# Talking-heads attention and squared-ReLU FFN on one core: reciprocals of row sums and pair copies on GpSimd, a post-mix buffer stored in runs of 35, and a new order of units

## The chip, the cores and the metric

The kernel runs on one core of one Trainium2 chip. The metric is the device time in microseconds of one execution; lower is better. Three executions of the kernel before took 535.64, 533.0 and 532.7 us, median 533.0 us.

## What is computed

Eight batches of talking-heads attention (12 heads, 448 rows, head size 64) are followed by one feed-forward layer (768 to 2048 to 768) over all 3584 rows.

```python
scores = scale * np.matmul(q, k.transpose(0, 1, 3, 2))
scores = np.einsum('bhij,hg->bgij', scores, w_pre)
scores = scores - np.max(scores, axis=-1, keepdims=True)
attn = np.exp(scores)
attn = attn / (np.sum(attn, axis=-1, keepdims=True) + 1e-09)
attn = np.einsum('bhij,hg->bgij', attn, w_post)
attn_out = np.matmul(attn, v)
x = attn_out.transpose(0, 2, 1, 3).reshape(B * S, H * D)
h = np.maximum(x @ w_in, 0.0)
out = h * h @ w_out
```

The heads are mixed before the softmax with `w_pre` and after it with `w_post`. These two mixes join all 12 heads of one query row, and they shape the kernel.

## The kernel before, in words

**Tiles.** The 448 query rows of a batch are cut into 45 chunks of 10 (`CH`), the last one with 8 valid rows. A chunk with its 12 heads is 120 rows, held as two groups of 60 (5 query rows by 12 heads, `PR`), one in partitions 0 to 63 and one in 64 to 127. Two chunks make a pair; a batch has 22 pairs and a lone chunk, so there are 184 such steps. The 448 keys are 7 tiles of 64: three double tiles of 128 keys (`NM`) and a tail of 64.

**The path of a batch.** DMAs bring q and k. For batches 1 to 7 a copy (`shf`, line 822, function `copy` at lines 480 and 481) puts the two heads of a pair next to each other, TensorE transposes them (line 807), and a copy brings them back out of PSUM. QK products (line 981) go through PSUM to `stage` in SBUF; DMAs of SP (`rel`, line 1026) move them from rows of queries to rows of query and head, into `dring`. The pre-mix (`pre`, line 1069 and two other forms) multiplies by `wk1`. ScalarE takes the exponential from PSUM into a slot of `pring` (10 slots, five pairs) with the sums of rows into `sums` (line 1107). Batch 0 reaches its first 22 chunks in another way (`dir`, line 922), with scaled copies of q.

**The step that is changed.** Once both exponentials of a pair are there, `rec` (line 1123, VectorE) takes the reciprocals of the sums, two numbers in each partition, into `rinv`. `fold` (line 1130) multiplies the post-mix weights by them into `wk2s`; for the first ten groups on VectorE, later on GpSimd. `tail` (line 1141) multiplies the 64 tail keys of both chunks by them into `ptail`; the first ten groups on VectorE, later on either (FLEX). `post` (line 1177) then runs 7 products for each of the two row groups, with the probabilities as the stationary and the 60 columns of weights as the moving operand, so that keys come to lie in the partitions. Their 420 columns are copied by ScalarE or VectorE (`a2ev`, line 1193) to `a2t`, which has for each of the two halves of a batch (22 and 23 chunks) the layout [block, head, query]: 84 runs of 5 numbers in each copy.

**AV and FFN.** `av` (line 1239) multiplies `vraw` by `a2t`, two heads at a time in column halves of the array, for three double tiles and twice for the tail (even rows with `vraw`, odd rows with `vodd`), 20 matmuls a unit and 48 units in all. What is streamed is a stretch of `a2t` with all queries of a half next to each other (two runs of 110 or 115, or one for a tail). `xtev` (line 1251) copies the result to `xt` in two copies, since even and odd row groups lie apart in PSUM. The first FFN product is at lines 1291 and 1312, the ReLU at 1343 and 1344, the square at 1353 (VectorE), the second product at 1433, and GpSimd issues the output DMAs (line 1466).

**The order.** TensorE's units lie in ten streams, and the string `ORDER` says from which stream the next unit comes (0 transposes, 1 QK, 2 pre, 3 post, 4 AV, 5 dir, 6 and 7 first product, 8 and 9 second product; a is a pre in row form, b one in column form, c a QK unit of 64 rows in row form). A planner goes through it with a cost for each step, places each FLEX step on the engine that ends first, and so fixes each engine's own order before the kernel is built. On the chip every engine then runs its list in that order and waits at semaphores. The planner's costs are pairs: how long the engine is held, and when the result is there, in ns.

```python
e = min(t.cost, key=lambda e: max(self.free[e], t.avail) + t.cost[e][1]
        + (ACT_BIAS if e == ACT else t.bias if e == DVE else 0.0))
```

PSUM has 8 banks, and a unit of TensorE needs one or two free ones. Steps marked `two` are booked as keeping VectorE off while GpSimd runs one.

Of the kernel before, what the change touches and what calls it, by code (L numbers as in the profile page):

```python
# [7 lines left out]
ALU = mybir.AluOpType  # L8
# [22 lines left out]
    "000101551c0055555555555555c15555551335555c13555555c1355c355555555300325555c3352002555300"  # L31
    "ccc32241c4a3343a7a3326763226673376ac377313616c36114447221662776c223776723c676c33673c713a"
    "6722293932293393a83c002800c3812800324242124c18cc1833381318132762cc7632663ac772266c337622"
    "44423376631377c11762210066722776333762138218217766200383338322780101822c8138c19313922293"
    "93224413931a93cc9133922244441226116c373a373361c62200722736236373217363360220711738220081"
    "c183c182224419333922393192228181138c338c3224244423263163371337226c16a37c1730062136007217"
    "3622167337224422009319c319cc192283382228383c933191a3931c9312422244428381138318a3613c6372"
    "200716212673376221673372200621673337a01091392229393183c181138c3c82224441c83a8a38c3382244"
    "422363c6c7317c61363722276ac63722176c0063700337228338221838310091c192229c9339c33913922298"
    "a318a38133831c4422244442217c37363c61631637222776c167336222673739112933939122444228338222"  # L40
    "8386338633822288733677a67767663376744486867677667766776879989998898899"
# [283 lines left out]
def bass_talking_heads_attention__then__ffn_squared_relu_kernel(  # L325
# [39 lines left out]
    NBK = 2 * NM + 1  # L365
# [6 lines left out]
    with ExitStack() as es:  # L372
# [35 lines left out]
        flag = sb("flag", [1, 1], DT.int32)  # L408
        rinv = sb("rinv", [128, NPS, 1], DT.float32)
# [11 lines left out]
        a2t = [sb("a2t%d" % i, [128, NBK, H, NG[i] * H5], DT.bfloat16) for i in range(2)]  # L421
        ptail = sb("ptail", [128, NPS // 2, 2, PJ], DT.bfloat16)
        vodd = sb("vodd", [128, H, D], DT.bfloat16)
        xt = sb("xt", [128, NP, NCH * CH], DT.bfloat16)
# [28 lines left out]
        def program(safe):  # L453
# [36 lines left out]
            def fn_init(eng, en):  # L490
                eng.memset(mask[:, :, :], 1.0)
                eng.memset(wk1r[:, :], 0.0)
                eng.memset(wk1c[:, :, :], 0.0)
                eng.memset(wrep[:, :], 0.0)
                eng.memset(wk2b[:, :, :], 0.0)
                return eng.memset(ident[:, :], 0.0)
# [284 lines left out]
            def emit_T(b):  # L781
                pb = b % 2
                for a in range(3):
                    g = _Group(2)
                    trs = []
                    for i, src in enumerate((qraw, kraw)):
# [26 lines left out]
                        if b:  # L813
                            def fn_shf(eng, en, a=a, i=i, src=src):
# [270 lines left out]
            def after_pre(g, t_pre, gr, x):  # L1085
# [36 lines left out]
                def fn_rec(eng, en):  # L1122
                    return eng.reciprocal(rinv[:, p0:p0 + n, :], sums[:, g0:g0 + n, :])  # L1123

                t_rec = add("rec%d_%d" % (b, c), DVE, fn_rec, [exp_of[g0], t_exp] + old_users(g),
                            {DVE: (82.0, 160.0)}, b * 1000.0 - 900 + c)

                def fn_fold(eng, en):
# [7 lines left out]
                             {POOL: (330.0, 370.0), DVE: (200.0, 280.0)},  # L1136
# [3 lines left out]
                def fn_tail(eng, en):  # L1140
# [15 lines left out]
            def emit_post(g0):  # L1156
# [558 lines left out]
```

## Time and profile before

| what | value |
|---|---|
| median of three runs | 533.0 us |
| the profiled execution, its own time | 532.63 us |
| its span, first to last instruction | 530.9 us |
| TensorE clock, mean | 0.999 of full |
| DMA | 72.06 MB, mean 136 GB/s |
| HBM read and written | 45.70 MB and 11.01 MB |

The span is 1.7 us shorter than the execution's own time. A line of a group gives the line of the code, the engine, the operation, the output and input with their shapes, the count, then the busy time and the mean duration of one, and the idle time of the engine just before them with what ended it. PE is TensorE, PEld its loading of weights, DVE VectorE, ACT ScalarE, POOL GpSimd. Matmuls overlap and their ends are modelled, so that starts are the surer reading.

### The profile page before, as it was taken

The page shows a single profiled execution, that of the slowest core. Times are in us where ns is not written, and L with a number is a line of the kernel's source. Part 1 is how long each engine was busy: PE and PEld are TensorE (multiplying, and loading weights), DVE is VectorE, ACT ScalarE, POOL GpSimd, SP SyncE. Part 2 cuts the span into 40 slices and gives each one's busy share as a digit, 9 for nine tenths or more (in the row PEclk, how much of TensorE's full clock was granted, in tenths as well). Part 3 has the DMA queues.
Part 4 walks back from the last instruction along what each step waited for, and adds up shares of the span by engine and source line. Part 5 has one row for each costly group of instructions (what it writes and reads, how often), then busy time and mean ns, then how long its engine had stood idle before and what let it go on. Part 6 is the DMA issues. An engine that isn't in the chain of part 4 may idle for free.

```text
span 530.9 us, 21923 instructions
## 1 busy us (share of the span) xinstructions
PE 511.9 (96%) x8876; PEld 321.6 (61%) x8876; DVE 431.3 (81%) x1181; ACT 453.0 (85%) x1282; POOL 233.5 (44%) x434
## 2 busy tenths in 40 slices
PE   7999999899999999999999999999999999999997
PEld 3545777567765664466546664456646575567874
DVE  7988878899998779978999788976899678877540
ACT  4789999899999999989999989989998898897421
POOL 9735445443663366434733357423663342233000
PEclk9999999999999999999999999999999999999999
DMA  9989979836795579546984689535894656652003
GB/s 178 199 172 188 205 129 204 191 92 138 147 183 125 129 148 174 117 91 152 183 149 97 142 163 169 124 84 121 166 162 100 139 129 113 120 116 64 3 19 106
DMA packets 82386, 72.06 MB, mean 136 GB/s; under 512 B 13370, under 2 KB 79530, under 8 KB 82282
## 3 DMA queue, kind: packets, MB, share of 16 engines
q0 software_dynamic: 36480, 32.58, 37.8%
q1 hardware_dynamic: 45514, 37.83, 29.5%
q8 instruction: 72, 1.18, 0.9%
q14 instruction: 32, 0.26, 0.1%
q10 hardware_dynamic: 288, 0.20, 0.1%
HBM read 45.70 MB, written 11.01 MB: 107 GB/s over the span
## 4 chain that ended last, share of the span: by engine, by line
PE 66%; DVE 14%; ACT 10%; DMA 6%; POOL 2%; issue 1%; DVEq 0%; ACTq 0%; POOLq 0%; SPq 0%
PE ps L1433 22%; PE ps L1312 14%; PE ps L1239 7%; PE ps L1069 5%; PE ps L1177 5%; PE ps L981 5%; PE ps L1291 4%; ACT a2t L480 3%; ACT pring L1107 3%; DVE stage L481 3%; DMA kraw<-in_k_dram 3%; DVE a2t L481 3%; DMA vraw<-in_v_dram 2%; DVE ptail L1141 2%; PE ps L1381 2%; DVE h2t L1353 2%
## 5 line engine op out<-in xcount | busy, mean ns | idle before, releaser
L1107 ACT ACTIVATE pring<-ps 128x448 bf16<-128x448 f32 (+1 forms) x368 | 196.6, 563 | 14.2 <-PE ps L1069 7.1
L1130 POOL TENSOR_TENSOR wk2s<-wk2b,rinv 128x120 bf16<-128x120 bf16 x179 | 76.2, 428 | 182.0 <-DVE rinv L1123 180.8
L1433 PE MATMUL ps<-w_out_sb,h2t 64*128 64x384 bf16 x1664 | 151.8, 323 | 0.1
L1312 PE MATMUL ps<-xt,w_in_sb 64*128 64x448 bf16 (+2 forms) x1344 | 122.8, 322 | 1.2 <-DVE qkt L481 0.9
L480 ACT ACTIVATE a2t<-ps 128x420 bf16<-128x420 f32 x185 | 113.0, 672 | 8.3 <-PE ps L1177 7.7
L481 DVE CAST a2t<-ps 128x420 bf16<-128x420 f32 x175 | 109.5, 651 | 8.2 <-PE ps L1177 7.5
L480 ACT ACTIVATE stage<-ps 128x448 bf16<-128x448 f32 (+1 forms) x198 | 102.7, 560 | 10.2 <-PE ps L981 8.9
L1433 PEld LDWEIGHTS ps<-w_out_sb,h2t 64*128 64x128 bf16 x1664 | 78.2, 94 | 49.2 <-PE ps L1069 2.2
L481 DVE CAST stage<-ps 128x448 bf16<-128x448 f32 (+1 forms) x162 | 97.1, 614 | 7.1 <-PE ps L981 5.4
L1312 PEld LDWEIGHTS ps<-xt,w_in_sb 64*128 64x128 bf16 x1344 | 61.2, 94 | 40.5 <-PE ps L1069 1.9
L1107 ACT ACTIVATION_READ_ACCUMULATOR pring<-ps 128x1 f32 (+1 forms) x368 | 83.7, 227 | 0.0
L1466 POOL DMA_DIRECT2D out_dram<-osb x52 | 33.6, 652 | 83.3 <-DVE osb L481 26.1
L1177 PEld LDWEIGHTS ps<-wk2s,pring 60*128 60x128 bf16 x2160 | 53.2, 93 | 27.9 <-DVE ptail L1141 2.3
L1177 PE MATMUL ps<-wk2s,pring 60*128 60x60 bf16 x2160 | 60.2, 187 | 4.4 <-POOL wk2s L1130 1.7
L1141 DVE TENSOR_TENSOR ptail<-pring,rinv 128x128 bf16<-128x128 bf16 x163 | 56.3, 346 | 1.7
L1353 DVE TENSOR_TENSOR h2t<-h1t 128x448 bf16<-128x448 bf16 (+2 forms) x176 | 53.5, 333 | 3.8 <-ACT h1t L1343 3.2
L981 PE MATMUL ps<-qkt 64*128 64x448 bf16 (+1 forms) x360 | 53.3, 355 | 1.4 <-DVE a2t L481 0.6
L1343 ACT ACTIVATE h1t<-ps 128x448 bf16<-128x448 f32 (+2 forms) x86 | 38.4, 460 | 17.3 <-PE ps L1312 14.7
L1344 DVE TENSOR_SCALAR h1t<-ps 128x448 bf16<-128x448 f32 (+2 forms) x90 | 42.8, 479 | 12.7 <-PE ps L1312 10.0
L1123 DVE RECIPROCAL rinv<-sums 128x2 f32<-128x2 f32 x184 | 28.8, 157 | 27.6 <-ACT pring L1107 27.1
L1069 PE MATMUL ps<-dring,wk1r 64*64 64x448 bf16 (+1 forms) x614 | 47.5, 364 | 2.7 <-DVE a2t L481 1.1
L1291 PE MATMUL ps<-xt,w_in_sb 128*128 128x228 bf16 (+1 forms) x384 | 42.2, 260 | 1.0 <-issue 0.8
(79 smaller groups left out, 596.2 us busy)
## 6 DMA issues: line engine op xcount, KB each, us to landing
dring<-stage SPq DMA_DIRECT2D x309, 105.0 KB
out_dram<-osb POOLq DMA_DIRECT2D x52, 192.0 KB, 3.7
qraw<-in_q_dram POOLq DMA_DIRECT2D x42, 112.0 KB, 5.8
kraw<-in_k_dram POOLq DMA_DIRECT2D x42, 112.0 KB, 5.3
w_in_sb<-in_moe_w_in_dram POOLq DMA_DIRECT2D x8, 384.0 KB, 10.1
vraw<-in_v_dram POOLq DMA_DIRECT2D x24, 128.0 KB
w_out_sb<-in_moe_w_out_dram POOLq DMA_DIRECT2D x8, 384.0 KB, 10.5
vraw<-in_v_dram POOLq DMA_DIRECT2D x24, 96.0 KB
```

The costliest lines, as they stand in the source:

```text
L480: return eng.activation(o, i_, AF.Copy)
L481: return eng.tensor_copy(o, i_)
L981: r_ = eng.matmul(ps[o:o + i_, g.banks[x], 0:S], qkt[r0:r0 + 64, pb, p_ % 3, 0, p_ // 3, i0 + w - i_:i0 + w], qkt[r0:r0 + 64, pb, p_ % 3, ...
L1069: r_ = eng.matmul(ps[64 * y:64 * y + 64, gr.banks[x], 0:S], wk1[64 * x:64 * x + 64 - R0 * x, :], dring[64 * x:64 * x + 64 - R0 * x, (g0 + ...
L1107: return eng.activation(pring[0:r1, pr, 0:S], ps[0:r1, gr.banks[x], 0:S], AF.Exp, accum_out=sums[0:r1, g, :], **bias)
L1130: return eng.tensor_tensor(wk2s[:, p0:p0 + n, :], i0.to_broadcast([128, n, PR]), rinv[:, p0:p0 + n, :].to_broadcast([128, n, PR]), ALU.mult)
L1141: return eng.tensor_tensor(ptail[:, p0 // 2, :, :], pring[:, p0:p0 + n, 0:PJ], rinv[:, p0:p0 + n, :].to_broadcast([128, n, PJ]), ALU.mult)
L1177: r_ = eng.matmul(ps[:, gr.banks[x], o * PR:(o + 1) * PR], p_, w_, start=True, stop=True)
L1291: r_ = eng.matmul(ps[:, g.banks[0], 0:n], w_in_sb[:, ft, t * 128:(t + 1) * 128], xt[:, ft, c0:c1], start=(ft == 0), stop=(ft == NFT - 1))
L1312: r_ = eng.matmul(ps[:, g.banks[x], 0:n], w_in_sb[64 * y:64 * y + 64, ft, t * 128:(t + 1) * 128], xt[64 * y:64 * y + 64, ft, c0:c1], start ...
L1353: return eng.tensor_tensor(h2t[:, t16, o0:o0 + n], h1t[:, s, 0:n], h1t[:, s, 0:n], ALU.mult)
L1433: r_ = eng.matmul(ps[:, g.banks[hh], 0:FH], h2t[64 * y:64 * y + 64, t16, col:col + 128], w_out_sb[64 * y:64 * y + 64, t16, hh * FH:(hh + 1 ...
```

## The change

Six things are changed together.

1. `rec` moves to GpSimd for all but the first ten groups, as a power with exponent -1 (a tensor of -1 is the second operand).
2. All `shf` copies go to GpSimd; before, the planner chose between VectorE and GpSimd.
3. `tail` stays FLEX after the first ten groups, but VectorE is charged 300 ns more in the choice, and the costs differ.
4. `a2t` is stored as [head, chunk, 36], with the seven blocks of 5 of a chunk and head next to each other: 12 runs of 35 in each copy, which now reads PSUM in runs of 5. The seven products of `post` change their order, so that the two row groups of a key tile follow each other.
5. `av` streams from this layout: for each chunk a run of 10 out of 36, for a tail a run of 5, and a tail's result goes to PSUM in runs of 5. The result has its queries in their order, so `xtev` is one copy, but for the first half of batch 0, where it is four.
6. `ORDER` is another string of the same 950 units. Some costs of the planner change with the rest.

```diff
--- before.py
+++ after.py
@@ -28,17 +28,17 @@
 INF = float("inf")
 STREAM = {"a": 2, "b": 2, "c": 1, **{str(i): i for i in range(10)}}
 ORDER = (
...
 )
 
 
@@ -362,7 +362,7 @@
     NCP = NCH + 1
     NM = NT // 2
     NG = tuple(-(-x // 2) * 2 for x in HC)
-    NBK = 2 * NM + 1
+    GW = (2 * NM + 1) * H5 + 1
     PARTS0 = ((0, HC[0]), (HC[0], NCH))
     PR = H5 * H
     R0 = 64 - PR
@@ -406,6 +406,7 @@
         nmax = sb("nmax", [128, NPS, 2], DT.float32)
         test = sb("test", [128, 4], DT.float32)
         flag = sb("flag", [1, 1], DT.int32)
+        minus = sb("minus", [128, 2, 1], DT.float32)
         rinv = sb("rinv", [128, NPS, 1], DT.float32)
         sb("align", [128, 16], DT.uint8)
         w_in_sb = sb("w_in_sb", [128, NFT, FF], DT.bfloat16)
@@ -418,10 +419,10 @@
         dring = sb("dring", [128, NDS, S], DT.bfloat16)
         osb = sb("osb", [128, 4, NOS, OP], DT.float32)
         pring = sb("pring", [128, NPS, S], DT.bfloat16)
-        a2t = [sb("a2t%d" % i, [128, NBK, H, NG[i] * H5], DT.bfloat16) for i in range(2)]
+        a2t = [sb("a2t%d" % i, [128, H, NG[i], GW], DT.bfloat16) for i in range(2)]
         ptail = sb("ptail", [128, NPS // 2, 2, PJ], DT.bfloat16)
         vodd = sb("vodd", [128, H, D], DT.bfloat16)
-        xt = sb("xt", [128, NP, NCH * CH], DT.bfloat16)
+        xt = sb("xt", [128, NP, S], DT.bfloat16)
         h1t = sb("h1t", [128, NH1, S], DT.bfloat16)
         h2t = sb("h2t", [128, NFFT, 512], DT.bfloat16)
         warm = sb("warm", [128, S], DT.bfloat16)
@@ -489,6 +490,7 @@
 
             def fn_init(eng, en):
                 eng.memset(mask[:, :, :], 1.0)
+                eng.memset(minus[:, :, :], -1.0)
                 eng.memset(wk1r[:, :], 0.0)
                 eng.memset(wk1c[:, :, :], 0.0)
                 eng.memset(wrep[:, :], 0.0)
@@ -819,9 +821,9 @@
                                         "p (t c d) -> p t c d", c=2, d=D),
                                     src[:, 2 * a:2 * a + 2, :, :].rearrange("p c t d -> p t c d"))
 
-                            t_shf = add("shf%d_%d_%d" % (b, a, i), FLEX, fn_shf,
+                            t_shf = add("shf%d_%d_%d" % (b, a, i), POOL, fn_shf,
                                         landed + [qk_done.get(b - 2)],
-                                        {DVE: (400.0, 500.0), POOL: (1500.0, 1620.0)},
+                                        {POOL: (990.0, 1050.0)},
                                         b * 1000.0 - 710)
                             t_shf.two = True
                             landed = [t_shf]
@@ -1120,10 +1122,14 @@
                 p0 = g0 % NPS
 
                 def fn_rec(eng, en):
+                    if en == POOL:
+                        return eng.tensor_tensor(rinv[:, p0:p0 + n, :], sums[:, g0:g0 + n, :],
+                                                 minus[:, 0:n, :], ALU.pow)
                     return eng.reciprocal(rinv[:, p0:p0 + n, :], sums[:, g0:g0 + n, :])
 
-                t_rec = add("rec%d_%d" % (b, c), DVE, fn_rec, [exp_of[g0], t_exp] + old_users(g),
-                            {DVE: (82.0, 160.0)}, b * 1000.0 - 900 + c)
+                t_rec = add("rec%d_%d" % (b, c), DVE if g < 10 else POOL, fn_rec,
+                            [exp_of[g0], t_exp] + old_users(g),
+                            {DVE: (82.0, 160.0), POOL: (130.0, 170.0)}, b * 1000.0 - 900 + c)
 
                 def fn_fold(eng, en):
                     i0 = wk2b[:, :, :].rearrange("p a b -> p (a b)").unsqueeze(1)
@@ -1133,7 +1139,7 @@
 
                 t_fold = add("fold%d_%d" % (b, c), DVE if g < 10 else POOL, fn_fold,
                              [t_rec, t_wk2] + old_users(g),
-                             {POOL: (330.0, 370.0), DVE: (200.0, 280.0)},
+                             {POOL: (344.0, 400.0), DVE: (200.0, 280.0)},
                              b * 1000.0 - 900 + c)
                 t_fold.two = True
 
@@ -1144,9 +1150,10 @@
 
                 t_tail = add("tail%d_%d" % (b, c), DVE if g < 10 else FLEX, fn_tail,
                              [t_rec, t_exp, exp_of[g0]] + old_users(g),
-                             {POOL: (390.0, 430.0), DVE: (210.0, 290.0)},
+                             {POOL: (350.0, 400.0), DVE: (200.0, 290.0)},
                              b * 1000.0 - 900 + c)
                 t_tail.two = True
+                t_tail.bias = 300.0
                 for y in members(g0):
                     fold_of[y] = t_fold
                     tail_of[y] = t_tail
@@ -1161,12 +1168,12 @@
                 pr = g0 % NPS
                 gr = _Group(n)
                 old = [av_of.get((b - 1, half))]
-                nb = NBK
+                nb = 2 * NM + 1
 
                 def fn_post(eng, en):
                     r_ = None
                     for o in range(nb):
-                        y, s = divmod(o, NM + 1)
+                        s, y = divmod(o, 2)
                         j0 = (2 * s + 1) * PJ
                         for x in range(n):
                             rows = slice(64 * x, 64 * x + PR)
@@ -1184,17 +1191,16 @@
                 for g in gs:
                     post_of[g] = t_post
                     a2_of[g] = []
-                k0 = (c0 - half * HC[0]) * H5
-
                 for x in range(n):
                     def fn_a2(eng, en, x=x):
-                        d = a2t[half][:, :, :, k0 + x * H5:k0 + (x + 1) * H5].rearrange(
-                            "p o h t -> p (o h) t")
-                        return copy(eng, en, d, ps[:, gr.banks[x], 0:nb * PR].rearrange(
-                            "p (o t) -> p o t", t=H5))
+                        d = a2t[half][:, :, c0 - half * HC[0] + x, 0:nb * H5].rearrange(
+                            "p h (o t) -> p h o t", t=H5)
+                        src = ps[:, gr.banks[x], 0:nb * PR].rearrange(
+                            "p (o h t) -> p h o t", h=H, t=H5)
+                        return copy(eng, en, d, src)
 
                     t_a2 = add("a2ev%d_%d" % (g0, x), FLEX, fn_a2, [t_post] + old,
-                               c_ev(nb * PR), b * 1000.0 - 800 + c0)
+                               {ACT: (408.0, 518.0), DVE: (506.0, 596.0)}, b * 1000.0 - 800 + c0)
                     for g in gs:
                         a2_of[g].append(t_a2)
                     gr.readers[x].append(t_a2)
@@ -1228,37 +1234,40 @@
                                 for kk in range(2):
                                     h = 2 * (p + x) + kk
                                     o_ = ps[kk * 64:kk * 64 + 64, g.banks[0], x * w:(x + 1) * w]
-                                    a_ = a2t[half][:, :, h, k0 * H5:k1 * H5]
-                                    if s < NM:
-                                        a_ = a_[:, s::NM + 1, :]
-                                        o_ = o_.rearrange("p (y n) -> p y n", y=2)
-                                    else:
-                                        a_ = a_[:, NM, :]
-                                        o_ = o_[:, (s - NM) * (w // 2):(s - NM + 1) * (w // 2)]
+                                    o_ = o_.rearrange("p (g c) -> p g c", c=CH)
                                     v_ = vraw[:, h, s, :] if s <= NM else vodd[:, h, :]
-                                    r_ = eng.matmul(o_, v_, a_,
+                                    i0, i1 = s * CH, (s + 1) * CH
+                                    if s >= NM:
+                                        i0, i1 = NM * CH, NM * CH + H5
+                                        u = (s - NM) * H5
+                                        o_ = o_[:, :, u:u + H5]
+                                    r_ = eng.matmul(o_, v_, a2t[half][:, h, k0:k1, i0:i1],
                                                     start=(s == 0), stop=(s > NM))
                         return r_
 
                     t_av = unit(s_AV, "av%d_%d_%d" % (b, c0, p), fn_av,
                                 a2 + v_of[b] + [odd_of[b]] + t_zero[:1],
-                                2 * NS * (w / 2.4 + 2.9) + 8.0, "cols", g, 4 * (NS + 1))
+                                2 * NS * (w / 2.4 + 2.9) + 78.0, "cols", g, 4 * (NS + 1))
 
                     def fn_x(eng, en, p=p, g=g):
+                        if (b, half) != (0, 0):
+                            return copy(eng, en, xt[:, p:p + 2, c0:c1],
+                                        ps[:, g.banks[0], 0:2 * w].rearrange(
+                                            "p (x n) -> p x n", x=2)[:, :, 0:n])
                         r_ = None
-                        m = CH if (b, half) == (0, 0) else H5
-                        for y in range(2):
+                        for x, y in QUADS:
                             r_ = copy(eng, en,
-                                      xt[:, p:p + 2, c0:c0 + w].rearrange(
-                                          "p x (k m) -> p x k m", m=2 * m)[:, :, :, y * m:y * m + m],
-                                      ps[:, g.banks[0], 0:2 * w].rearrange(
-                                          "p (x y k t) -> p x y k t", x=2, y=2, t=m)[:, :, y])
+                                      xt[:, p + x, c0:c1].rearrange(
+                                          "p (k c x t) -> p k c x t", c=2, x=2, t=H5)[:, :, y],
+                                      ps[:, g.banks[0], x * w:(x + 1) * w].rearrange(
+                                          "p (k x c t) -> p k c x t", c=2, x=2, t=H5)[:, :, y])
                         return r_
 
+                    ev = c_ev(2 * n)
+                    if (b, half) == (0, 0):
+                        ev = {e: (h_ + 330.0, l_ + 330.0) for e, (h_, l_) in ev.items()}
                     t_x = add("xtev%d_%d_%d" % (b, c0, p), FLEX, fn_x,
-                              [t_av] + f1_of.get((b - 1, half), []),
-                              {e: (h_ + 90.0, l_ + 90.0) for e, (h_, l_) in c_ev(2 * w).items()},
-                              b * 1000.0 - 850)
+                              [t_av] + f1_of.get((b - 1, half), []), ev, b * 1000.0 - 850)
                     xtev[(b, part)].append(t_x)
                     g.readers[0].append(t_x)
                 if part[1] in (HC[0], NCH):
```

More of the change, by code (lines that the diff above doesn't have):

```diff
@@ L30 @@
 ORDER = (
[L31 to L41, printed above, removed]
+    "000c0c551c005555555c5555555555ccc555555133555551c155555533355553325555300002255535551100"
+    "331c3c412b4433322766a3a613622763373c622777633317711c44b432266766227677113c67633372267116"
+    "7c2293393229383c9001282180032803302244b43c283118cc38ccc833663222677a17763c3a766331176224"
+    "422477113762c36633327663117630102762227766211838128333803022772283a8003831181c93119c3c92"
+    "2392244a93119c33931392224444cca6cc16a73337a3a63c6003722276a363373a7362126733700381128001"
+    "8ccc8c22442c9223933933c9228c381ca81338221342244422363c6137ca73363c62271c7a3006336217a370"
+    "0621167337224422009339111911c9222838133813382239a19c1393c3922244422248318318c3c810306226"
+    "37c3733622267c37a633600721276221673373c9300192229c9831183138c1c8222443813a833813c8222444"
+    "422363367117c161361722276336721276300a6373217008223833821280092239c19c339119ca3931392229"
+    "8a38c338ccc8c334422244442226736c736317c6317633c6c722276226733739121933939122444222838338"
+    "22288338322836836637a6776763378674447667766776677676787689989999998888"
 )
```

## The prediction

> **What bounds the kernel now.** I read the page first, then the busy time by stretch, then the waits, the groups by shape, and last TensorE's own timeline. The page gives the span, the busy time of the engines, and the chain that ended last by engine.
>
> ```profile
> span 530.9 us, 21923 instructions
> PE 511.9 (96%) x8876; PEld 321.6 (61%) x8876; DVE 431.3 (81%) x1181; ACT 453.0 (85%) x1282; POOL 233.5 (44%) x434
> PE 66%; DVE 14%; ACT 10%; DMA 6%; POOL 2%; issue 1%; DVEq 0%; ACTq 0%; POOLq 0%; SPq 0%
> ```
>
> TensorE is busy for 511.9 of 530.9 us, so what is added to its own work adds to the time, and 19.0 us are idle to be seen. Yet it holds only 66% of the chain: a quarter (14% and 10%) runs through VectorE and ScalarE, which empty its PSUM banks. Busy time by stretch (columns: length, PE, PEld, DVE, ACT, POOL, clock, DMA share, GB/s) shows where the idle time lies.
>
> ```profile
> 0.00:25.00 25.00, 21.04 (x281) 11.00 (x282) 20.75 (x67) 14.03 (x35) 20.18 (x36) 1.00 1.12 187
> 25.00:100.00 75.00, 70.07 (x1120) 45.55 (x1118) 61.84 (x192) 69.01 (x209) 36.00 (x64) 1.00 0.97 180
> 100.00:300.00 200.00, 195.95 (x3563) 123.56 (x3557) 178.30 (x473) 189.79 (x541) 94.46 (x180) 1.00 0.68 139
> 300.00:500.00 200.00, 197.56 (x3589) 122.09 (x3586) 162.44 (x426) 174.31 (x487) 80.34 (x151) 1.00 0.60 122
> 500.00:531.00 31.00, 27.31 (x344) 19.43 (x338) 7.98 (x26) 5.83 (x14) 2.53 (x4) 0.98 0.21 53
> ```
>
> Start and end hold 7.6 us of TensorE's idle time, which the change hardly touches. From 25 to 500 us it is 4.93 + 4.05 + 2.44 = 11.4 us, most of it where ScalarE is at 92 to 95% and VectorE at 82 to 89%. From 100 us on, three engines are near their end at once. The clock is full, so it plays no part. The waits (total, times, longest) say who is late for whom.
>
> ```profile
> POOL wk2s L1130 <- DVE rinv L1123: 180.8, 124, 7.0
> DVE rinv L1123 <- ACT pring L1107: 27.1, 33, 1.9
> POOL qkt L481 <- DMA kraw<-in_k_dram: 7.5, 8, 2.9
> POOL qkt L481 <- DMA qraw<-in_q_dram: 4.8, 3, 3.1
> PEld ps L1069 <- DVE a2t L481: 4.1, 11, 0.8
> PEld ps L981 <- ACT stage L480: 2.2, 8, 0.5
> PEld ps L1177 <- DVE ptail L1141: 2.3, 2, 2.0
> PE ps L1177 <- POOL wk2s L1130: 1.7, 1, 1.7
> ```
>
> TensorE's waits are many and short, and behind copies out of PSUM. GpSimd's idle time is 180.8 us in front of the fold alone, so it has room. The post-mix matmuls (L1177) wait for a fold or a tail three times in 184, for 4.0 us in all: rows of exponentials are finished well ahead of their use.
>
> **The copies and the reciprocals.** The groups by shape (count | busy us, mean ns | idle before):
>
> ```profile
> L480 ACT ACTIVATE a2t<-ps 128x420 bf16<-128x420 f32 x185 | 113.0, 672 | 8.3 <-PE ps L1177 7.7
> L481 DVE CAST a2t<-ps 128x420 bf16<-128x420 f32 x175 | 109.5, 651 | 8.2 <-PE ps L1177 7.5
> L480 ACT ACTIVATE stage<-ps 128x448 bf16<-128x448 f32 x159 | 82.0, 566 | 9.0 <-PE ps L981 8.3
> L481 DVE CAST stage<-ps 128x448 bf16<-128x448 f32 x117 | 69.7, 613 | 6.2 <-PE ps L981 5.4
> L481 DVE CAST xt<-ps 128x220 bf16<-128x220 f32 x40 | 13.7, 388 | 5.1 <-PE ps L1239 5.0
> L480 ACT ACTIVATE xt<-ps 128x230 bf16<-128x230 f32 x28 | 9.6, 429 | 0.8 <-PE ps L1239 0.5
> L1123 DVE RECIPROCAL rinv<-sums 128x2 f32<-128x2 f32 x184 | 28.8, 157 | 27.6 <-ACT pring L1107 27.1
> L481 DVE COPY qkt<-qraw 128x896 bf16<-128x896 bf16 x13 | 7.9, 606 | 0.0
> L481 DVE COPY qkt<-kraw 128x896 bf16<-128x896 bf16 x6 | 3.7, 614 | 0.5 <-DMA kraw<-in_k_dram 0.5
> L481 POOL COPY qkt<-kraw 128x896 bf16<-128x896 bf16 x15 | 14.8, 990 | 7.5 <-DMA kraw<-in_k_dram 7.5
> L1141 DVE TENSOR_TENSOR ptail<-pring,rinv 128x128 bf16<-128x128 bf16 x163 | 56.3, 346 | 1.7
> L1141 POOL TENSOR_TENSOR ptail<-pring,rinv 128x128 bf16<-128x128 bf16 x21 | 8.4, 399 | 0.0
> L1130 POOL TENSOR_TENSOR wk2s<-wk2b,rinv 128x120 bf16<-128x120 bf16 x179 | 76.2, 428 | 182.0 <-DVE rinv L1123 180.8
> ```
>
> *a2t.* A plain copy of 448 columns takes 566 ns on ScalarE and 613 on VectorE; less 28 columns (at one a cycle, 1.2 and 0.96 in a ns by the planner's own slopes) that is 543 and 584 for 420. The a2t copies, which write runs of 5, take 672 and 651: 129 and 67 ns more for 84 runs, or 1.5 and 0.8 ns a run. The new copy writes 12 runs of 35 and instead reads PSUM in runs of 5. If only the writing cost, 185 x 129 + 175 x 67 = 23.9 + 11.7 = 35.6 us of busy time go. If reading in runs of 5 costs as much as writing did, nothing goes; at twice that price 35.6 us come on top. No row has such a read. I take the first, because the one row pair that I have puts the price on the write; the other ends lead to the case without relief below.
>
> *xt.* Two copies of about 220 become one of about 440, nearly the 448-column row: on VectorE 2 x 388 - 613 = 163 ns, on ScalarE 2 x 429 - 566 = 292 ns. The 40 + 20 VectorE and 28 + 8 ScalarE halves make about 30 and 18 units: 4.9 + 5.3 = 10 us. In the first half of batch 0, two copies of each unit become four, three times, which is some 2 us.
>
> *rec.* Of 184 reciprocals 179 leave VectorE (those of the first ten row groups, five pairs, stay): 28 us of busy time, and with them the 27.1 us in which VectorE's queue stood before them, with the evictions queued behind. GpSimd shows no power and nothing of two elements. The price is between VectorE's row of the same shape (157 ns) and the 240-element fold (428), 28 to 77 us; I take 160 ns, since the fold pays for its elements. The fold then waits for its own engine, but the tail on VectorE now waits for GpSimd, and a2t and stage copies queue behind that tail.
>
> *shf and tails.* The 13 + 6 pair copies move: 11.6 us off VectorE, 19 x 0.99 = 18.8 on GpSimd. The copies wait at the head of its queue for DMAs to land, and now recs, folds, tails and output DMA issues stand behind 42 of them, not 23. Tails are placed by the planner, 300 ns in favour of GpSimd: anything from 21 to 179; I take some 70 more, 24 us off VectorE and 28 on GpSimd.
>
> Together VectorE loses 11.7 + 4.9 + 28 + 11.6 + 24 = 80 us and ScalarE 23.9 + 5.3 = 29, 12% of their 884; GpSimd goes to 233.5 + 29 + 19 + 28 = 309 us (58%), or 357 (67%) at the dear power. None of it is time until TensorE waits less for it.
>
> **TensorE's own work.** Its timeline (start us, length us) near 420 us:
>
> ```profile
> 419.97 1.47 PE L1433 MATMUL ps<-w_out_sb,h2t 64*128 64x384 bf16 x16
> 421.36 0.76 PE L1069 MATMUL ps<-dring,wk1r 64*64 64x448 bf16 x12
> 422.06 2.77 PE L1433 MATMUL ps<-w_out_sb,h2t 64*128 64x384 bf16 x32
> 424.67 0.54 PE L1054 MATMUL ps<-dring,wk1r 64*128 64x448 bf16 x4
> 425.05 0.25 PE L1177 MATMUL ps<-wk2s,pring 60*128 60x60 bf16 x6
> ...
> 433.30 0.52 PE L1239 MATMUL ps<-a2t,vraw 128*64 128x220 bf16 x8
> 433.65 0.22 PE L1239 MATMUL ps<-a2t,vodd 128*64 128x110 bf16 x2
> 433.70 0.50 PE L1239 MATMUL ps<-a2t,vraw 128*64 128x220 bf16 x8
> 434.03 0.22 PE L1239 MATMUL ps<-a2t,vodd 128*64 128x110 bf16 x2
> 434.08 0.52 PE L1239 MATMUL ps<-a2t,vraw 128*64 128x230 bf16 x8
> ```
>
> Starts are to be read, since ends are modelled. Ahead of the same array shape (64-row tiles) a second-FFN unit takes 2.61 / 2 = 1.30 us; ahead of the 64x64 shape it takes 1.39. A change of shape costs 0.09 us. Read against the lists of units, the old order changes shape 247 times and the new one 218 times: 29 x 0.09 = -2.6 us. It pays for that with slower forms: a pre-mix pair is 0.38 us in the row form (424.67 to 425.05) and (0.70 - 0.09) / 3 = 0.20 in quads. Pairs in row form go from 12 to 16, three come in the column form (the same four streams, two at a time, so the same price), and one 64-row QK unit fewer is in row form: 6 x 0.18 = +1.1 us.
>
> An AV unit takes 434.08 - 433.30 = 0.78 us. Its 1760 columns, streamed for two heads at once, stay, but what is streamed comes in runs of 10, and the tails in runs of 5 that also land in PSUM in runs of 5. No matmul of this trace does that. Below zero is excluded, as nothing is streamed less. Above, 2 x (3 x 22 + 2 x 22) = 220 runs at ScalarE's 1.5 ns would be 0.33 us a unit, 48 units 16 us; at VectorE's 0.8 ns 8 us. The diff books 70 ns a unit (78 for 8). Its AV book was 765 ns for 220 columns where the rows show 780, so I take its 70: 48 x 0.07 = +3.4 us, unhidden. The sum of TensorE's own work is -2.6 + 1.1 + 3.4 = +1.9 us.
>
> The Trainium skill, in PSUM — Partial Sum Buffer, Specifications, speaks against this: 8-byte lines, and any non-contiguous pattern slows matmuls significantly. It gives no price, and no run here shows it yet; it is the first rival below.
>
> **The relief.** The pool is the 11.4 us of idle TensorE from 25 to 500 us, and a part that modelled ends cover: the unit above is drawn 1.47 us long where the next could start at 1.30. I take that part to be as large again, an estimate: 23 us. A queue at 95% that loses 12% of its work waits far less than in proportion, but busy time on ScalarE overlaps and GpSimd gets later. I take somewhat under half, 10 us; bounds 0 and 23. Next late is then TensorE itself.
>
> Sum: 1.9 - 10 = -8.1 us on the profiled execution's 532.63 us (span 530.9, 1.7 around it) gives 524.5; the median of the runs, 533.0, is 0.4 above that execution, so 525.
>
> **The rivals.** *Short runs stall AV (slower).* At ScalarE's price a run, AV costs 16.2 us instead of 3.4: 525 + 12.8 = 538. It decides from 11.5 us, 240 ns a unit. For it: the a2t rows, where short runs cost both engines. Against: that is another engine's write path. If only the tails' PSUM writes went at half speed (4 x 110 columns, at 0.78 us for 1760), it is 0.19 us a unit and 9 us in all, 6 more than the sum has: 531. The skill's PSUM rule would act in this way.
>
> *GpSimd becomes late (slower).* Today 11 of 23 pair copies stood 12.3 us for a landing; 42 would stand 22 us, with all recs behind. If the power costs 428 ns and half of the 22 us reaches TensorE through tails that block VectorE, it is +11: 536. It decides from 8 us. Against: posts waited 4.0 us in all, and 180.8 us of slack.
>
> *No relief (no change).* TensorE at 96% gains nothing from freer engines, only its own +1.9: 535. For it: its waits are short and spread.
>
> **How the numbers follow.** About 0.5%, 2.7 us, can be told from no change. Forecast 0.66, no relief 0.14, AV 0.10, GpSimd 0.10. The forecast's own range is 516 (relief 19) to 530; with no relief and most of GpSimd's case it is 516 to 536. Faster is the forecast, 0.66; same is no relief and AV's half case, 0.16; slower 0.18.
>
> **What would show it.** a2t rows near 543 and 584 ns, xt as one copy near 600; no RECIPROCAL after the first pairs, a row on GpSimd that writes rinv at 130 to 200 ns; GpSimd near 310 us; AV units near 0.85 us from start to start; TensorE's idle time from 25 to 500 us near 6 us. AV units over 1.0 us, or long waits of L1177 or of ptail for GpSimd, would prove me wrong; so would a2t copies still near 660.

## The result, and the profile after

The changed kernel takes 578.25 us (median of four runs, 574.96 to 579.83) against 533.67 us for the kernel before (four runs): 1.0822 times as long, with a 95% interval of 1.076 to 1.0885. The forecast was 525 us, within 516 to 536. The profiled execution took 574.96 us. The page of the changed kernel: span, busy time, and the chain that ended last by engine.

```profile
span 573.2 us, 21881 instructions
PE 526.6 (92%) x8876; PEld 331.4 (58%) x8876; DVE 397.3 (69%) x909; ACT 441.0 (77%) x1260; POOL 400.2 (70%) x690
PE 39%; POOL 35%; DVE 10%; ACT 9%; issue 3%; DMA 3%; DVEq 0%; POOLq 0%
```

VectorE lost 34 us of busy time and ScalarE 12, where the forecast had 80 and 29. GpSimd gained 167 and went from 2% of the chain to 35%. TensorE is idle for 46.6 us where it was idle for 19.0, and its busy time grew by 14.7 us, of which AV's units make 7.3 (below). The groups by shape of the changed kernel (count | busy us, mean ns of one | idle before) show the power, which makes 127.5 of the 167 us, and the tails and copies.

```profile
L1126 POOL TENSOR_TENSOR rinv<-sums,minus 128x2 f32<-128x2 f32 x179 | 127.5, 714 | 53.9 <-ACT pring L1109 52.9
L1147 DVE TENSOR_TENSOR ptail<-pring,rinv 128x128 bf16<-128x128 bf16 x105 | 37.9, 361 | 96.6 <-POOL rinv L1126 96.5
L481 ACT ACTIVATE a2t<-ps 128x420 bf16<-128x420 f32 x188 | 91.6, 532 | 29.0 <-PE ps L1184 27.9
L482 DVE CAST a2t<-ps 128x420 bf16<-128x420 f32 x172 | 97.3, 590 | 10.5 <-PE ps L1184 9.9
L482 DVE CAST xt<-ps 128x440 bf16<-128x440 f32 x18 | 11.0, 613 | 8.9 <-PE ps L1244 8.8
```

A power of two numbers in each partition takes 714 ns on GpSimd, where the reciprocal took 157 on VectorE and the planner books 130 to 170. The copies came out as foreseen: 532 and 590 ns for a2t, 613 for xt. The second row is the new wait: VectorE stands 96.5 us at its tails, which stood 1.7 us before. The waits of the changed kernel (total, times, longest) go on from there.

```profile
DVE ptail L1147 <- POOL rinv L1126: 96.5, 93, 2.8
POOL rinv L1126 <- ACT pring L1109: 52.9, 29, 10.0
POOL qkt L482 <- DMA qraw<-in_q_dram: 5.6, 4, 3.1
POOL qkt L482 <- DMA kraw<-in_k_dram: 5.0, 4, 2.2
PE ps L1184 <- DVE stage L482: 9.2, 16, 1.9
PE ps L983 <- DVE stage L482: 4.2, 4, 2.9
```

TensorE hardly waits for GpSimd itself. Added up over all rows of its waits, it stands 4.4 us for GpSimd and 32.9 us for VectorE, mostly for copies out of PSUM; before, it stood 7.4 us for VectorE. These copies stand in VectorE's queue behind a tail which waits for the power: for 27 of the 32.9 us, a wait of a tail for the power ended during TensorE's wait or at most 1.5 us before it. One instance, on the timeline of the changed kernel (start, length; in brackets the idle time before and what ended it):

```profile
276.11 0.72 POOL L1126 TENSOR_TENSOR rinv<-sums,minus 128x2 f32<-128x2 f32 x1
276.86 0.29 DVE L1147 TENSOR_TENSOR ptail<-pring,rinv 128x128 bf16<-128x128 bf16 x1 [2.40 <-POOL rinv L1126]
277.07 0.59 DVE L482 CAST a2t<-ps 128x420 bf16<-128x420 f32 x1
277.81 0.35 PE L1184 MATMUL ps<-wk2s,pring 60*128 60x60 bf16 x12 [1.60 <-DVE a2t L482]
278.22 0.94 ACT L481 ACTIVATE a2t<-ps 128x420 bf16<-128x420 f32 x2 [1.61 <-PE ps L1184]
```

The power ends at 276.83, the tail starts at once, the a2t copy behind it frees a bank at 277.66, and only then can TensorE go on. ScalarE in turn has nothing to copy for 1.61 us: a late engine makes its neighbours idle, and their lower busy time is no relief.

### The profile page after: what moved, and what is told of

It is laid out like the page before. It is cut to its first block, busy times and chain, and to the rows that moved or that the text cites. A ratio compares the mean times of both kernels' runs of the same rounds, so it can differ in the third digit from the quotient of the medians.

```text
span 573.2 us, 21881 instructions
## 1 busy us (share of the span) xinstructions
PE 526.6 (92%) x8876; PEld 331.4 (58%) x8876; DVE 397.3 (69%) x909; ACT 441.0 (77%) x1260; POOL 400.2 (70%) x690
## 4 chain that ended last, share of the span: by engine, by line
PE 39%; POOL 35%; DVE 10%; ACT 9%; issue 3%; DMA 3%; DVEq 0%; POOLq 0%
PE ps L1442 16%; POOL rinv L1126 13%; PE ps L1321 8%; POOL wk2s L1136 6%; ACT pring L1109 5%; POOL vraw L701 4%; PE ps L1184 4%; DVE stage L482 3%; PE ps L983 3%; POOL out_dram L1475 3%; POOL ptail L1147 2%; POOL kraw L663 2%; POOL qkt L482 2%; DMA vraw<-in_v_dram 2%; PE ps L1244 2%
## 5 line engine op out<-in xcount | busy, mean ns | idle before, releaser
L1109 ACT ACTIVATE pring<-ps 128x448 bf16<-128x448 f32 (+1 forms) x368 | 195.0, 551 | 19.4 <-PE ps L1071 10.5
L1126 POOL TENSOR_TENSOR rinv<-sums,minus 128x2 f32<-128x2 f32 x179 | 127.5, 714 | 53.9 <-ACT pring L1109 52.9
L481 ACT ACTIVATE a2t<-ps 128x420 bf16<-128x420 f32 x188 | 91.6, 532 | 29.0 <-PE ps L1184 27.9
L1147 DVE TENSOR_TENSOR ptail<-pring,rinv 128x128 bf16<-128x128 bf16 x105 | 37.9, 361 | 96.6 <-POOL rinv L1126 96.5
L482 DVE CAST a2t<-ps 128x420 bf16<-128x420 f32 x172 | 97.3, 590 | 10.5 <-PE ps L1184 9.9
L1109 ACT ACTIVATION_READ_ACCUMULATOR pring<-ps 128x1 f32 (+1 forms) x368 | 79.4, 216 | 0.0
L1184 PEld LDWEIGHTS ps<-wk2s,pring 60*128 60x128 bf16 x2160 | 49.0, 94 | 45.4 <-DVE stage L482 13.7
L1362 DVE TENSOR_TENSOR h2t<-h1t 128x448 bf16<-128x448 bf16 (+2 forms) x176 | 63.0, 386 | 4.0 <-ACT h1t L1352 3.3
L1353 DVE TENSOR_SCALAR h1t<-ps 128x448 bf16<-128x448 f32 (+2 forms) x98 | 46.8, 485 | 14.3 <-PE ps L1321 12.2
L1244 PE MATMUL ps<-a2t,vraw 128*64 128x220 bf16 (+3 forms) x768 | 47.5, 264 | 0.0
L1071 PE MATMUL ps<-dring,wk1r 64*64 64x448 bf16 x586 | 43.6, 362 | 1.1 <-issue 0.4
```

What stands on the lines that cost most here:

```text
L481: return eng.activation(o, i_, AF.Copy)
L482: return eng.tensor_copy(o, i_)
L1109: return eng.activation(pring[0:r1, pr, 0:S], ps[0:r1, gr.banks[x], 0:S], AF.Exp, accum_out=sums[0:r1, g, :], **bias)
L1126: return eng.tensor_tensor(rinv[:, p0:p0 + n, :], sums[:, g0:g0 + n, :], minus[:, 0:n, :], ALU.pow)
L1184: r_ = eng.matmul(ps[:, gr.banks[x], o * PR:(o + 1) * PR], p_, w_, start=True, stop=True)
L1244: r_ = eng.matmul(o_, v_, a2t[half][:, h, k0:k1, i0:i1], start=(s == 0), stop=(s > NM))
```

## The experiments

Theory A: the duration of the power, in its place between the exponential and the tail, is the loss. Theory B: any reciprocal on GpSimd loses, since VectorE's queue then depends on another. Theory C: AV's short runs and the new order are the loss.

**The changed kernel with the reciprocals on VectorE** (e1_rec_dve).

```diff
-                t_rec = add("rec%d_%d" % (b, c), DVE if g < 10 else POOL, fn_rec,
+                t_rec = add("rec%d_%d" % (b, c), DVE, fn_rec,
```

> The changed kernel with the reciprocals back on VectorE; everything else of the change stays (a2t in runs of 35, pair copies on GpSimd, the new order). Theory A, the price of the power: 714 ns on GpSimd in front of each fold and tail is what costs the time, so this takes back all of it and shows what the other parts are worth: 525 to 534 us, VectorE's wait of ptail for rinv gone (96.5 us to under 5). Theory B, the hop: any reciprocal on GpSimd hurts because tails of VectorE then stand for another engine's queue: the same 525 to 534 here. Theory C, AV's short runs and the new order cost it: 565 us or more, for nothing of them is taken back.

It took 539.1 us, 1.0108 times the kernel before (1.0048 to 1.0168). About seven of the eight per cent are gone, against theory C. But the rest of the change is not the gain that was forecast: it costs 1%. Its busy times:

```profile
PE 516.8 (97%) x8879; PEld 329.9 (62%) x8879; DVE 413.2 (77%) x1075; ACT 437.7 (82%) x1264; POOL 274.9 (51%) x520
```

VectorE and ScalarE are 33 us lighter than before in all, and still TensorE, busy for 516.8 us of a span of 534.4, is idle for 17.6 us, against 19.0. The relief hardly arrives.

**The kernel before with the power alone** (e2_before_pow).

```diff
...
+                    if en == POOL:
+                        return eng.tensor_tensor(rinv[:, p0:p0 + n, :], sums[:, g0:g0 + n, :],
+                                                 minus[:, 0:n, :], ALU.pow)
...
-                t_rec = add("rec%d_%d" % (b, c), DVE, fn_rec, [exp_of[g0], t_exp] + old_users(g),
-                            {DVE: (82.0, 160.0)}, b * 1000.0 - 900 + c)
+                t_rec = add("rec%d_%d" % (b, c), DVE if g < 10 else POOL, fn_rec,
+                            [exp_of[g0], t_exp] + old_users(g),
+                            {DVE: (82.0, 160.0), POOL: (130.0, 170.0)}, b * 1000.0 - 900 + c)
```

> The kernel before with one part of the change alone: the reciprocals after the first ten groups as a power on GpSimd, booked at the same 130 to 170 ns. Old a2t, old order, old places of copies and tails. Theories A and B: most of the loss is here, 560 to 585 us, with a wait of VectorE's ptail for GpSimd's rinv of 90 us or more (more tails than in the changed kernel stay on VectorE). Theory C: 533 to 540 us.

It took 575.68 us, 1.0786 (1.0734 to 1.0838): this one part makes nearly the whole loss. Its largest wait in total is the same one:

```profile
DVE ptail L1147 <- POOL rinv L1126: 102.0, 134, 2.7
```

**A multiplication in place of the power** (e3_mult_for_pow). It leaves out the reciprocal, so the rows are not normalised.

```diff
-                                                 minus[:, 0:n, :], ALU.pow)
+                                                 minus[:, 0:n, :], ALU.mult)
```

> The changed kernel with a multiplication by -1 in place of the power, on GpSimd, same shape and place: the rows are not normalised, and the numbers that come out are others. It keeps the hop to GpSimd and takes away the power's own time. I expect the instruction at 130 to 200 ns, as it was booked, against 714. Theory A: 525 to 536 us and ptail's wait for rinv under 25 us. Theory B: the hop alone costs, 555 us or more. Theory C: 565 or more.

It took 537.96 us, 1.007 (1.0034 to 1.0106), as much as with the reciprocals on VectorE. The groups of its page and its waits:

```profile
L1126 POOL TENSOR_TENSOR rinv<-sums,minus 128x2 f32<-128x2 f32 x179 | 37.9, 213 | 92.9 <-ACT pring L1109 91.9
```

```profile
DVE ptail L1147 <- POOL rinv L1126: 40.8, 58, 2.2
```

The same shape in the same place takes 213 ns, so 500 of the 714 ns are the power's own, and they are worth 40 us of time. VectorE still waits 40.8 us for GpSimd, more than the 25 that I expected, but that costs nothing that can be seen: TensorE stands 9.2 us for VectorE instead of 32.9, and only 1 us of them behind such a wait of a tail. Theory B falls: at 213 ns it is not the hop. Between the two profiles the span differs by 37.2 us; 26.7 of them are idle time of TensorE, and 10.5 are longer busy time of the same matmuls, which was not followed up.

**The power booked at its true duration** (e4_booked_right).

```diff
-                            {DVE: (82.0, 160.0), POOL: (130.0, 170.0)}, b * 1000.0 - 900 + c)
+                            {DVE: (82.0, 160.0), POOL: (690.0, 760.0)}, b * 1000.0 - 900 + c)
```

> The changed kernel with the planner's cost of the power corrected from 130 and 170 to 690 and 760 ns; the power itself stays on GpSimd. The planner then lays out the queues of VectorE and GpSimd for the true duration. Theory A has two forms. If a wrong book is the loss (VectorE's tails placed too early in its queue, evictions behind them): 535 to 548 us, ptail's wait for rinv under 30 us. If the load on GpSimd and the longer way to the fold are the loss: 560 us or more. Theory C: 565 or more.

It took 569.09 us, 1.0648 (1.0594 to 1.0702). A right book is worth 9 us. Its waits show that it works and where the time went instead:

```profile
DVE ptail L1147 <- POOL rinv L1126: 22.7, 37, 2.1
PE ps L809 <- POOL qkt L482: 15.9, 8, 3.9
PE ps L1184 <- DVE ptail L1147: 3.0, 2, 2.4
```

VectorE's wait shrinks from 96.5 to 22.7 us, and TensorE's transposes now wait 15.9 us for the pair copies, which stand in GpSimd's queue among the powers. In all TensorE stands 11.8 us for VectorE and 17.2 us for GpSimd, where it was 32.9 and 4.4. The loss is moved, not mended.

**The same powers as load alone** (e9_spare_pow).

```diff
...
+                if g >= 10:
+                    def fn_extra(eng, en):
+                        return eng.tensor_tensor(spare[:, p0:p0 + n, :], sums[:, g0:g0 + n, :],
+                                                 minus[:, 0:n, :], ALU.pow)
+
+                    t_extra = add("extra%d_%d" % (b, c), POOL, fn_extra, [t_fold],
+                                  {POOL: (130.0, 170.0)}, b * 1000.0 - 900 + c + 0.5)
```

> The kernel before with the same 179 powers on GpSimd as extra work: reciprocals stay on VectorE, and after each fold GpSimd computes a power into a tile that nobody reads. The same load on GpSimd as in e2_before_pow, but out of the path from the exponential to the fold and the tail. If the load is the loss (copies, folds and DMA issues late in a full queue): 560 us or more, as with e2_before_pow (575.7). If the place in the path is the loss (VectorE's tail standing for the power, evictions behind it): 533 to 542 us.

It took 545.34 us, 1.0233 (1.0181 to 1.0286), a little over the range of one theory and far below the other's. Its busy times and the wait in front of its folds:

```profile
PE 517.1 (95%) x8876; PEld 322.0 (59%) x8876; DVE 435.6 (80%) x1188; ACT 456.9 (84%) x1287; POOL 353.2 (65%) x602
```

```profile
POOL wk2s L1133 <- DVE rinv L1126: 90.7, 56, 5.8
```

With GpSimd nearly as full as in e2_before_pow (353.2 us against 360.0; 233.5 before), the load costs 2.3% where the same instructions in the path cost 7.9%. So somewhat under a third is the load, and the rest the place. The 180.8 us that GpSimd stood before its folds were not all free: 120 us more work took 90.1 of them, and still 12 us of time. The run also speaks against another rival, that VectorE is held up whenever a power runs beside it: its a2t copies take 652 ns here and 651 before.

**The layout alone, and all without it** (e5_layout_only, e6_no_layout). The first is the kernel before with items 4 and 5 of the change, the second has items 3 and 6 and the pair copies of item 2, with reciprocals and `a2t` as before. The first as an edit of the changed kernel, with the old string for ORDER, then the second as an edit of the kernel before, with the new one (the planner's costs of folds, tails and pair copies go with the string):

```diff
...
-                t_rec = add("rec%d_%d" % (b, c), DVE if g < 10 else POOL, fn_rec,
+                t_rec = add("rec%d_%d" % (b, c), DVE, fn_rec,
...
-                            t_shf = add("shf%d_%d_%d" % (b, a, i), POOL, fn_shf,
+                            t_shf = add("shf%d_%d_%d" % (b, a, i), FLEX, fn_shf,
...
-                t_tail.bias = 300.0
```

```diff
...
-                            t_shf = add("shf%d_%d_%d" % (b, a, i), FLEX, fn_shf,
+                            t_shf = add("shf%d_%d_%d" % (b, a, i), POOL, fn_shf,
...
+                t_tail.bias = 300.0
```

> The kernel before with the new a2t alone (12 runs of 35 in the copy, AV streaming runs of 10 and 5, xt in one copy), the old order, reciprocals on VectorE, pair copies and tails as before. The run with all of the change but the power (e1_rec_dve) came out 1% slower than before. Theory P: AV's short runs cost TensorE more (7.1 us between starts in the trace, 0.15 us a unit) than freer copies give back: 535 to 541 us here. Theory Q: the layout gains and it is the new order or the pair copies on GpSimd that lose: 525 to 533 us.

> The change without its two losers: reciprocals on VectorE and the old a2t, AV and xt; the new order, pair copies on GpSimd and the push of tails to GpSimd stay. Theory P: TensorE's AV units are back at 0.78 us and the other parts help a little: 526 to 532 us. Theory Q: 536 us or more.

The first took 545.19 us, 1.0207 (1.017 to 1.0245); the second 532.19, 0.9976 (0.9944 to 1.0009). Theory P holds in its direction for the first, where the layout is dearer than it said; the second lies at the upper end of its range and can't be told from the kernel before. The new order, the pair copies on GpSimd and the tails there make no difference that can be told, though they move 19 copies and 79 more tails. Busy time over the span, before and after the change (length; PE, PEld, DVE, ACT): the first view has all instructions on `a2t`, the second those of AV's line alone, which are all of TensorE's on `a2t`:

```profile
sum 531.00, PE 41.66 PEld 38.42 DVE 109.47 ACT 113.03; mean PE 8.33 PEld 7.68 DVE 21.89 ACT 22.61
```

```profile
sum 575.00, PE 49.00 PEld 45.03; mean PE 9.80 PEld 9.01
```

AV costs 7.3 us more, 0.15 us a unit. That is most of the 11.7 us that e5_layout_only lost (533.49 in its set); the other 4 were not followed up. With the new order the same layout costs 7 us (539.1 against 532.2, from two sets of runs).

**What in AV costs it** (e7_tail_psum_whole, e8_av_read_whole). Both start from e1_rec_dve; the first writes the tails to PSUM in one stretch, at rows where they do not belong; the second streams one stretch of the same length, of other numbers than it should.

```diff
...
-                                        o_ = o_[:, :, u:u + H5]
+                                        o_ = ps[kk * 64:kk * 64 + 64, g.banks[0],
+                                                x * w + (s - NM) * (w // 2):
+                                                x * w + (s - NM + 1) * (w // 2)]
```

```diff
...
+                                    m_ = (k1 - k0) * (i1 - i0)
+                                    a_ = a2t[half][:, h, :, :].rearrange("p g c -> p (g c)")
-                                    r_ = eng.matmul(o_, v_, a2t[half][:, h, k0:k1, i0:i1],
+                                    r_ = eng.matmul(o_, v_, a_[:, 0:m_],
```

> e1_rec_dve with AV's tail products written to PSUM in one stretch instead of runs of 5 (they land at the wrong rows, so the output is another); what is streamed stays in runs of 10 and 5. If the runs of 5 in PSUM are what slows the tails, a tail pair goes from about 70 ns between starts to about 50 and a 220-column unit from 0.93 us to 0.85; if the broken read does it, it stays at 0.93.

> e1_rec_dve with AV streaming one unbroken stretch of a2t of the same length for every product (other numbers than it should, so the output is another); the tails still land in PSUM in runs of 5. If the broken read is the whole price, an AV unit is back at 0.78 us; if the PSUM runs are the price of the tails, it is 0.85 us, with the products of whole rows back at 92 ns a pair.

Their times, one run each (540.83 and 544.63 us), tell nothing here; AV's busy time does. In this order: e1_rec_dve, e7_tail_psum_whole, e8_av_read_whole.

```profile
sum 550.00, PE 48.98 PEld 45.01 DVE 107.18 ACT 83.78; mean PE 48.98 PEld 45.01 DVE 107.18 ACT 83.78
```

```profile
sum 550.00, PE 49.38 PEld 45.38 DVE 107.27 ACT 83.78; mean PE 24.69 PEld 22.69 DVE 53.63 ACT 41.89
```

```profile
sum 550.00, PE 44.09 PEld 40.52 DVE 107.80 ACT 83.95; mean PE 22.05 PEld 20.26 DVE 53.90 ACT 41.98
```

Whole PSUM writes save nothing, so the broken read alone is enough for the whole price. A whole read saves 4.9 us of the 7.3, or 0.10 us a unit. With the read whole, the runs of 5 in PSUM still show: 44.09 against 41.66, 0.05 us a unit. So the two prices do not add: the broken read makes all of it alone and hides the broken write where both are there.

**A right book for the a2t copy** (e10_no_layout_booked on e6_no_layout, e11_before_booked on the kernel before).

```diff
-                               c_ev(nb * PR), b * 1000.0 - 800 + c0)
+                               {ACT: (480.0, 640.0), DVE: (520.0, 630.0)}, b * 1000.0 - 800 + c0)
```

> e6_no_layout with the planner's cost of the a2t copy set near the measured one (ScalarE 480 and 640 ns, VectorE 520 and 630, where it books 415 and 525, 509 and 597). If the copies that come out later than booked are what still holds TensorE up: 525 to 529 us, and clearly faster than before. If the order of the units was found for the other book and the waits only move: 531 to 535.

> The kernel before with only that book corrected, nothing else. If a right book helps by itself: 527 to 531 us; if not, 532 to 536.

They took 533.58 us, 0.9989 (0.9964 to 1.0015), and 536.21, 1.0057 (1.002 to 1.0094). Late copies are not what holds the kernel, or the string of units has to be found anew for each book; the two were not told apart. No version run here is clearly faster than the kernel before.

## Why the prediction was wrong

**The step that failed** is the price of the reciprocal: "between VectorE's row of the same shape (157 ns) and the 240-element fold (428), 28 to 77 us; I take 160 ns, since the fold pays for its elements." It measured 714 ns and 127.5 us, far outside both ends. (The fold's row has 120 numbers in each partition, not 240, which changes nothing here.) The argument on elements was nearly right: a product of the same two numbers takes 213 ns. But neither row was a power, and rows of another operation bound nothing. 500 ns belong to the operation, and no row of the trace before held it.

**The slack.** I counted 180.8 us of idle GpSimd as room and "180.8 us of slack" against the rival. e9_spare_pow shows that out of the path 128 us of powers cost 2.3%, and e2_before_pow that in the path they cost 7.9%. I named the mechanism (the tail on VectorE now waits for GpSimd, and the evictions stand behind it), put it at nothing in the sum and at +11 us in a rival. Long waits of ptail for GpSimd, which I named as a sign of being wrong, came true with 96.5 us.

**The rival that came true** was GpSimd becoming late, at 0.10. Its tails that block VectorE are what was seen. Its price was not: it had 428 ns for the power and +11 us, and it looked for the delay in copies that wait for landings, which fell from 12.3 to 10.6 us (5.6 and 5.0).

**The relief** was 10 us in the sum, from 109 us less work on VectorE and ScalarE. I had added up durations of rows, and those did fall: over all instructions of the two engines they went from 1111.4 to 1009.1 us, 102 less. But instructions of one engine overlap (on the timeline above the tail lasts until 277.15 and the copy behind it starts at 277.07), so their busy time fell by only 46 us. Even that gave nothing: e1_rec_dve has 33 us less busy time on the two and TensorE's idle time falls by 1.4 us. e3_mult_for_pow, where GpSimd's step costs nearly what I took, is at 538 us and not at 525: even with the right price of the power the forecast would have missed, and "no relief" was the true rival for the rest of the change: its 535 us with AV's measured price, 3.9 us over the one in the sum, make 539. Why lighter copies bring so little was not tested further. A quarter of the chain on VectorE and ScalarE did not mean that lighter copies shorten it.

**AV** was put at 0.07 us a unit after the diff's own book; it is 0.15 and 7.3 us, inside the bounds of 0 and 16. The Trainium skill's rule on non-contiguous patterns, in PSUM — Partial Sum Buffer, Specifications, has the direction right, but by e7_tail_psum_whole and e8_av_read_whole the runs in PSUM cost 0.05 us a unit where the read is whole, and nothing that shows beside the broken read.

**Right** were the durations of the copies (543 and 584 ns forecast for a2t, 532 and 590 measured; xt at 613), though no row had shown that only the writing of short runs costs, and the rows that vanish from VectorE. GpSimd stays below full, at 400.2 us, but above even the 357 of the dear power; it holds 35% of the chain while it is busy for 70% of the span.

## What to carry to other kernels

An operation that no row shows has no upper bound from rows of other operations: measure it alone, or hold the forecast open upwards. An engine's idle time is at best in part room for work off the path (2.3% was lost here); work in the path between two engines costs its latency (7.9%), and the step to look at is the first in-order queue that stands behind it. Durations of rows, added up, overstate what leaves an engine whose instructions overlap. Where the bounding engine reads a buffer, a layout that helps the engines which write it has to be priced by the reader first.

## What the runs showed of the hardware

In these traces TensorE's clock falls after a stretch of waits. The changed kernel between 276 and 285 us (length; PE busy, granted clock, DMA share, GB/s):

```profile
276.00:277.00 1.00, 0.21 (x4) 1.00 0.82 101
277.00:278.00 1.00, 0.19 (x14) 1.00 1.08 123
278.00:279.00 1.00, 0.18 (x13) 1.00 1.10 171
279.00:280.00 1.00, 0.63 (x8) 1.00 0.97 169
280.00:281.00 1.00, 1.00 (x8) 0.50 1.03 184
281.00:282.00 1.00, 1.00 (x8) 0.50 0.80 169
282.00:283.00 1.00, 1.00 (x8) 0.50 0.72 144
283.00:284.00 1.00, 1.00 (x18) 0.79 0.78 127
284.00:285.00 1.00, 1.00 (x38) 1.00 1.02 186
```

After 4 us in which it worked 1.2, it ran at half its clock for some 3.4 us (three rows at 0.50, and 0.4 us of the row at 0.79), which is up to 1.7 us of work lost on top of the wait in front of the a2t copy above. The same trace has a second such stretch: from 226 to 229 us it worked 1.3 of 3 us, and the rows from 228 to 233 show clocks of 0.90, 0.50, 0.50, 0.50 and 0.89, again 3.4 us at half. The Trainium skill, TensorE: Matmul & The Clock Gate, Part 1, gives half rate after an idle window and a window of about 3.4 us; the trace agrees in the length, though TensorE was not wholly idle. The four runs of the changed kernel had mean clocks of 0.994, 0.989, 0.984 and 0.982 at 574.96, 576.99, 579.83 and 579.52 us. The missing clock times the span, 3.4 to 10.4 us, is an estimate of what it cost; TensorE's idle time grew by more, 27.6 us in the profiled execution.

A run of 10 bf16 numbers in what TensorE streams is not free: by e8_av_read_whole a whole read takes back 0.10 us of a unit's 0.15. The Trainium skill, SBUF — State Buffer, Specifications, speaks of 16-byte lines: at least two hits in each give full bandwidth, and a crossing to a new line pays. These runs lie 72 bytes apart and start on multiples of 4 bytes of the tile, so they have two numbers or more in each line that they touch; by the first half of the rule they would be free, and the trace goes against that. The second half fits in its direction, since 20 bytes from such a start always lie in two lines where eight numbers of an unbroken stretch share one. Whether the crossings make the price, or the start of each new run does, no run here tells.
